# Packed attention with a mixture-of-experts layer: the expert's guess summed on GpSimd, one w2 conversion moved, a branch hint on SyncE, counts read behind the pair turn's copy

## The chip, the cores and the metric

One core of one Trainium2 chip. The metric is the device time in microseconds, the median of several runs; an execution's profile gives its span and what each engine did in it.

## The reference

```python
def sm_attn(qq, kk, vv):                       # per batch (8) and head (8)
    s = scale * qq @ kk.T; s -= s.max(-1)
    a = exp(s); a /= a.sum(-1) + 1e-9
    return a @ vv
packed = sm_attn(p, k, v)                      # 32 packed rows from 576 keys, D = 64
x = sm_attn(q, packed, packed)                 # 576 queries on the 32 packed rows
x = x.transpose(0, 2, 1, 3).reshape(4608, 512)
logits = unit(x) @ unit(expert_emb).T / tau    # 8 experts
e = argmax(logits, axis=1); gate = softmax(logits)[e]
out = gate * (relu(x @ w1[e]) @ w2[e])         # w1: 512 x 1024, w2: 1024 x 512 of expert e
```

All in float32, each token by its own expert.

## The kernel before

The kernel takes the 8 batches (576 tokens each) one after the other and runs two of them interleaved: while TensorE computes the feed-forward products of batch b (`ffn`), steps of the attention of batch b+1 (`att_main`) are put between them. All engines get their instructions in the order in which the Python program emits them (`tc.manual_schedule()`): `ffn` is a generator that yields after each small group of matmuls, and at each yield the main loop runs one step (now and then two) of `att_main(b + 1)` and, from step 21 on, of `gates`. So a step's place in the order of every engine's queue is a matter of how many yields stand ahead of it.

For each batch one expert is guessed: the sum of the packed rows' logits votes, `guess` takes the largest, and its w1 and w2 are loaded for the whole batch. `route` then computes every token's true expert, `counts` how many chose which, and `hits` takes those that chose the guess (`x.sel`) off the batch's 576. At the end all engines load the number of tokens left over (`n_rest`) and branch over a slow second pass (`tc.If(n_rest > 0)`, L1565), which does not run for these inputs. SyncE's branch stands behind its last store.

Weights are used as two parts in a rounded format: `split_w2` makes them by a ScalarE copy (L945) and a GpSimd subtraction (L946), for eight slices of w2 per batch. Four of them are made in the last quarter of the feed-forward product of the batch before (`c == 3`, from `f = 4` on), four in the second half of the hidden layer's steps.

The order of a batch's steps in `ffn` is: hidden layer (L1040, evacuated by ScalarE L1044 and VectorE L1045), the last rows (`h4`, L1075, eight yields, steps 16 to 23), then four groups `c` of 24 matmuls (L1093; group 3 in batch 7 in two halves) with stores. Between them stand, for the next batch: `quarter_scores` (L331), `quarter_values` (L396), the pair turn (L501) and its copy into `x.T` (L570), the row logits (L512, copied by L521), the guess (L631 and the lines behind it, `choose` below), the flips of keys and queries (L291), the query scores (L270), the softmax (`unpack` L677, `biggest` L682, `shift` L688, `total` L697 to L699, `norm` L703, `turn` L706, `low` L717), `route` (L772), and `w1_rows` (L970). `low(0)` runs on GpSimd in batches 2 to 7 ("vvvvpv"). GpSimd's queue also issues the loads of w1 (L927) and w2 (L935) for these batches. `gates` (L889 to L916, with `rsqrt`, L92 to L108) runs on VectorE.

Of the kernel before, what the change touches and what calls it, by code (L numbers as in the profile page):

```python
# [27 lines left out]
def kernel(  # L28
# [54 lines left out]
    ecol = cp.tile([P, E], F32, name="ecol")  # L83
    for e in range(E):
        nc.vector.memset(ecol[:, e : e + 1], float(e))
    rest_f = cp.tile([1, B], F32, name="rest_f")
    rest_i = cp.tile([1, B + 1], I32, name="rest_i")

    def rsqrt(x, y, tag, eng=nc.vector):

        i = sm.tile(list(x.shape), I32, name="rq_i", tag=f"rq_i{tag}", bufs=1)
        nc.vector.tensor_scalar(  # L92
            out=i, in0=x.bitcast(I32), scalar1=-0.5, scalar2=float(0x5F3759DF),
            op0=ALU.mult, op1=ALU.add,
        )
        yield
        hx = sm.tile(list(x.shape), F32, name="rq_h", tag=f"rq_h{tag}", bufs=1)
        eng.tensor_scalar_mul(hx, x, -0.5)
        yield
        t = sm.tile(list(x.shape), F32, name="rq_t", tag=f"rq_t{tag}", bufs=1)  # L100
        cur = i.bitcast(F32)
        for _ in range(3):
            eng.tensor_tensor(out=t, in0=hx, in1=cur, op=ALU.mult)
            yield
            eng.tensor_tensor(out=t, in0=t, in1=cur, op=ALU.mult)
            yield
            if eng is nc.vector:
# [145 lines left out]
    def idle(n):  # L253
        for _ in range(n):
            yield
# [157 lines left out]
    def quarter_sums(x, sums):  # L413
        t = sm.tile([P, NG], F32, name="qr", tag="qr", bufs=1)
        nc.vector.tensor_reduce(t, sums, axis=AX.X, op=ALU.add)
        nc.vector.tensor_scalar(out=t, in0=t, scalar1=1e-9, scalar2=None, op0=ALU.add)
        nc.vector.reciprocal(t, t)
        for g in range(NG):
            x.rinv[g] = t[:, g : g + 1]
# [108 lines left out]
    def att1(x, nat, queries=None, others=()):  # L528

        def pack(queries, others):  # L530
# [23 lines left out]
                counts(other, pt[:1, 256 + n * NC5 * E : 256 + (n + 1) * NC5 * E])  # L554
            next(queries)
            yield
            for other in others:
                counted(other)
                if other is bat[0]:
                    hits(0)  # L560
            quarter_sums(x, sums.rearrange("p (g k) -> p g k", g=NG))
            for g in range(NG):
                pair_rows(x, g, pt[:, g * D : g * D + D])
# [4 lines left out]
            for g in range(NG):  # L568
                pair_turn(x, g, pu)
            nc.vector.tensor_copy(x.T, pu[:, 0 : NG * P])  # L570
            yield from idle(2)
            pt = pc.tile([P, 512], F32, name="pu", tag="pu")
            row_logits(x, pt)
            yield
            logits_out(x, pt)
            next(queries)
            yield

# [39 lines left out]
                drain(asked)  # L618


    def guess(x, late=0, engine=mybir.EngineType.Pool, total=None):
# [12 lines left out]
        yield  # L634
        m8 = sm.tile([1, 8], F32, name="m8", tag="m8", bufs=1)
        idx = sm.tile([1, 8], U32, name="idx", tag="idx", bufs=1)
        nc.vector.max(m8, pt[:1, :E])
        nc.vector.max_index(idx, m8, pt[:1, :E])
# [6 lines left out]
        yield from idle(late)  # L645
        x.e = nc.values_load(
            idx[0:1, 0:1], engines=[engine], min_val=0, max_val=E - 1,
            skip_runtime_bounds_check_because="an index of the largest of E columns",
        )


    def att2(x, after=None, first=False, b1=False, eng1="vvvvvv"):
# [73 lines left out]
        def softmax():  # L726
            order = (
                (unpack, 0), (biggest, 0), (shift, 0), (unpack, 1), (biggest, 1), (total, 0),
                (shift, 1), (norm, 0), (turn, 0), (total, 1), (low, 0), (norm, 1), (turn, 1),
            )  # L730
            if x is bat[1]:
                order = (
# [256 lines left out]
    def ffn(x, store, late=False, after=None, end=False, between=None):  # L989
# [96 lines left out]
        for c in range(4):  # L1086

            w = 256 if end and c == 3 else 512
            for at in range(0, 512, w):
                pf = ps.tile([P, 512], F32, name="pf", tag="pf")  # L1090
                for f in range(NF):
# [8 lines left out]
                    yield  # L1100
                    if f == STF and len(last) > late or f == STF + 3 and late and c == 2:
                        store(*last.pop(0))
                    if c == 3 and f >= 4 and after is not None:
                        split_w2(after)
                    if c == AHEAD and hasattr(after, "lg") and not hasattr(after, "w1g"):
                        after.w1g = w1_rows(after)
# [48 lines left out]
    def att_main(b):  # L1155
        x = bat[b]
        if b:
            if b > 1:
                quarter_banks(x)
            queries = all_queries(x, nat_main(b)) if b > 1 else None  # L1160
            yield from att1(x, nat_main(b), queries, bat[b - 1 if b > 2 else 0 : b] if b > 1 else ())
            sync = b == 1
            queue = nc.sync if sync else nc.gpsimd
            for n, _ in enumerate(guess(
                x, 0 if sync else 2, mybir.EngineType.SP if sync else mybir.EngineType.Pool
            )):
                if n == 1 and queries:
                    next(queries)
                yield
            load_w1(x, x.e, queue=queue)  # L1170
        flips = keys_main(b + 1) if b else None
        second = att2(x, flips, b == 0, b < 1, ENG1 if b == 1 else "vvvvpv")
        if b:
            if b > 1:
                yield
            for _ in range(3 if b == 1 else 2):
                yield next(second)
            load_w2(x, x.e, queue)
        yield from second
        x.soft = True  # L1180
        if b:
            steps = {"r": route(x), "f": flips}
            if b == 1:
                next(flips)
            for turn in TURNS:
                for step in turn:
                    next(steps[step], None)
                yield
        if b == B - 1:
            yield from idle(2)  # L1190
            counts(x)

    def begin():
# [161 lines left out]
        nc.vector.tensor_copy(total, pt[:, :NPR])  # L1355
        both_rows(1)
        queries(0, 0, nc.scalar.copy)
        g_guess = guess(x, 0, mybir.EngineType.SP, total)
        next(g_guess)
        pu = bank()  # L1360
        for g in range(NG):
# [78 lines left out]
    def store_main(b):  # L1440
        x = bat[b]

        def store(c, pf, at, w):
            o = sb.tile([P, DM], F32, name="o", tag="o", bufs=3)
            nc.scalar.activation(o[:, :w], pf[:, :w], AF.Copy, scale=x.gate[:, c : c + 1])  # L1445
            if b == 0:

                for a in range(HB):
# [3 lines left out]
                        rs[:, hf * w + at : hf * w + at + w], o[32 * a : 32 * a + 32, :w]  # L1452
                    )
                return
            rs = out_rows(b, c)
            for a in range(HB):
                n, hf = (a, 0) if c < 4 else (a % 2, a // 2)
# [104 lines left out]
    nc.vector.tensor_reduce(tot, rest_f, axis=AX.X, op=ALU.add)  # L1562
    nc.vector.tensor_copy(rest_i[:, B : B + 1], tot)
    n_rest = nc.values_load(rest_i[0:1, B : B + 1], min_val=0, max_val=B * S)
    with tc.If(n_rest > 0):  # L1565
        with tc.For_i(0, B, 1) as b:
            nb = nc.values_load(rest_i[0:1, ds(b, 1)], min_val=0, max_val=S)
            with tc.If(nb > 0):
# [86 lines left out]
```

## Time and profile before

| | |
|---|---|
| runs | 416.88 us median of 3 (416.35 to 417.67) |
| profiled execution | 416.72 us, span 415.1 us, clock 0.998 |
| busy | PE 403.9 us, PEld 326.1, DVE 307.2, ACT 203.4, POOL 156.7 |
| DMA | 87.93 MB, mean 212 GB/s |

PE is TensorE's matmul side, PEld its weight loads, DVE VectorE, ACT ScalarE, POOL GpSimd, SP SyncE. Times in the views are microseconds from the span's start; "idle before" is the time an engine stood still ahead of a row and what released it. Waits, branches and DMA issues are not counted as busy (a "q" behind the engine's name).

### The profile page before, as it was taken

What the parts mean: (1) busy time and instruction counts of PE and PEld (TensorE: products, weight loads), DVE (VectorE), ACT (ScalarE), POOL (GpSimd) and SP (SyncE); (2) the same over time, 40 slices, a digit from 0 to 9 for tenths busy, and PEclk for the clock granted to TensorE, in tenths of its full rate; (3) what the DMA queues carried; (4) which work ended last, traced back from release to release, by engine and by line L of the source; (5) the groups of instructions that cost most, each with busy time, mean ns of one, the idle gap of its engine ahead of it and who ended that gap; (6) DMA issues with size and microseconds to landing.
All of it is one profiled execution on the core that took longest, in us unless ns stands there. A gap on an engine that the chain in (4) does not pass through costs nothing.

```text
span 415.1 us, 11135 instructions
## 1 busy us (share of the span) xinstructions
PE 403.9 (97%) x4036; PEld 326.1 (79%) x4037; DVE 307.2 (74%) x977; ACT 203.4 (49%) x507; POOL 156.7 (38%) x196
## 2 busy tenths in 40 slices
PE   7999999999999999999999999999999999999993
PEld 3758688797868978698787978689786988779783
DVE  3677889588977889779896889778896798736500
ACT  4677355762357703764147622666038631576110
POOL 2345802437204561056414471046512473142200
PEclk9999999999999999999999999999999999999999
DMA  8999798966989579986999779895899819310021
GB/s 230 334 333 233 205 289 277 238 178 180 309 276 233 144 209 260 308 209 166 247 334 247 183 199 286 302 224 140 236 299 284 199 34 353 119 51 2 20 53 51
DMA packets 42608, 87.93 MB, mean 212 GB/s; under 512 B 11690, under 2 KB 20906, under 8 KB 42546
## 3 DMA queue, kind: packets, MB, share of 16 engines
q1 hardware_dynamic: 35280, 61.44, 53.9%
q0 software_dynamic: 6720, 25.17, 18.9%
q8 instruction: 34, 0.56, 0.6%
q10 hardware_dynamic: 546, 0.54, 0.6%
q14 instruction: 28, 0.23, 0.2%
HBM read 77.68 MB, written 9.44 MB: 210 GB/s over the span
## 4 chain that ended last, share of the span: by engine, by line
PE 92%; DVE 2%; DMA 2%; ACT 1%; POOL 1%; issue 0%; SPq 0%; DVEq 0%; ACTq 0%; POOLq 0%
PE pf L1093 43%; PE pf L1040 23%; PE pf L1075 7%; PE pt L970 3%; PE pt L772 3%; PE pt L270 2%; PE pt L396 2%; PE pt L331 2%; PE pu L772 2%; DMA nat<-in_k 1%; PE pf L1235 1%; PE pt L1267 1%; PE pt L464 1%; DVE hT L1045 0%; PE pf L477 0%
## 5 line engine op out<-in xcount | busy, mean ns | idle before, releaser
L1093 PE MATMUL pf<-w2s,hT 128*128 128x512 f32 (+1 forms) x792 | 181.8, 387 | 0.0
L1093 PEld LDWEIGHTS pf<-w2s,hT 128*128 128x128 f32 x792 | 143.8, 188 | 39.0 <-issue 10.9
L1040 PE MATMUL pf<-AT,G 128*128 128x288 f32 x720 | 102.1, 299 | 0.4 <-DVE hT L1045 0.3
L1040 PEld LDWEIGHTS pf<-AT,G 128*128 128x128 f32 x720 | 97.2, 188 | 4.3 <-issue 1.5
L946 POOL TENSOR_TENSOR w2s<-w2r,w2s 128x512 fp32r<-128x512 f32 x64 | 80.6, 1285 | 50.0 <-ACT w2s L945 50.0
L1045 DVE SCALAR_TENSOR_TENSOR hT<-pf,hT 128x224 fp32r<-128x224 f32 (+1 forms) x128 | 52.3, 414 | 29.9 <-ACT hT L1044 29.6
L1044 ACT ACTIVATE hT<-pf 128x224 fp32r<-128x224 f32 (+1 forms) x128 | 49.2, 385 | 42.8 <-PE pf L1040 40.2
L291 DVE STREAM_TRANSPOSE kt<-nat 128x576 f32<-128x576 f32 x52 | 38.8, 764 | 1.3 <-DMA nat<-in_q 0.6
L1445 ACT ACTIVATE o<-pf,gate 128x512 f32<-128x512 f32 (+1 forms) x41 | 25.9, 633 | 25.7 <-PE pf L1093 14.4
L945 ACT CAST w2s<-w2r 128x512 fp32r<-128x512 f32 x64 | 37.1, 627 | 0.0
L717 POOL TENSOR_TENSOR AT<-at,AT 128x576 fp32r<-128x576 f32 x8 | 11.4, 1421 | 62.2 <-ACT AT L712 62.2
L1075 PE MATMUL pf<-w2r,h 128*64 128x256 f32 x256 | 32.9, 387 | 0.0
L691 ACT ACTIVATE st<-st 128x576 f32<-128x576 f32 (+1 forms) x17 | 11.1, 657 | 37.5 <-DVE st L688 36.4
L983 DVE TENSOR_TENSOR G<-pt,G 128x1024 fp32r<-128x1024 f32 x14 | 16.5, 1220 | 15.7 <-ACT G L982 15.7
L908 ACT ACTIVATE lg<-lg 128x40 f32<-128x40 f32 x8 | 1.9, 236 | 50.7 <-DVE lg L904 50.7
L1075 PEld LDWEIGHTS pf<-w2r,h 128*64 128x64 f32 x256 | 19.5, 137 | 5.1 <-PE pu L501 1.1
L866 POOL MEMSET oh<- 64x8 f32 x8 | 0.8, 98 | 58.5 <-DVE oh L862 58.5
L383 POOL TENSOR_TENSOR qs<-p 128x320 f32<-128x320 f32 x12 | 10.5, 878 | 30.2 <-ACT p L364 30.2
L785 ACT ACTIVATE scr<-pt 128x512 f32<-128x512 f32 (+1 forms) x32 | 15.7, 491 | 12.6 <-DVE part L826 5.8
L712 ACT CAST AT<-at 128x576 fp32r<-128x576 f32 x15 | 10.1, 674 | 23.3 <-DVE at L706 23.2
L364 ACT ACTIVATE p<-pt,qnm 128x160 f32<-128x160 f32 x48 | 17.7, 398 | 0.0
L703 DVE TENSOR_TENSOR st<-st,s 128x576 f32<-128x576 f32 x14 | 16.8, 1202 | 0.3
(229 smaller groups left out, 513.8 us busy)
## 6 DMA issues: line engine op xcount, KB each, us to landing
nat<-in_q SPq DMA_DIRECT2D x112, 140.0 KB, 3.4
nat<-in_k SPq DMA_DIRECT2D x96, 140.0 KB, 4.2
w1t<-in_moe_w POOLq DMA_DIRECT2D x12, 1024.0 KB, 9.7
w2r<-in_moe_w POOLq DMA_DIRECT2D x24, 512.0 KB, 15.8
out<-o SPq DMA_DIRECT2D x124, 64.0 KB, 2.1
w2r<-in_moe_w SPq DMA_DIRECT2D x8, 512.0 KB, 9.7
vn<-in_v SPq DMA_DIRECT2D x24, 160.0 KB, 3.6
vn<-in_v SPq DMA_DIRECT2D x48, 80.0 KB, 3.8
```

Of the source, the lines that this page charges most:

```text
L291: nc.vector.transpose(kt.rearrange("p (c i) -> p c i", i=32), t)
L364: nc.scalar.activation(x.p1[g][:, n * QW : n * QW + QW], area(x, g)[:, n // 2, n % 2], AF.Exp, bias=x.nm[:, at : at + 1],)
L703: eng("N", hf).tensor_tensor(out=t, in0=t, in1=spread(sums[hf], gs), op=ALU.mult)
L772: nc.tensor.matmul(to, x.at[at, g, tokens], x.ppx[at, g], start=True, stop=True, tile_position=(64 * half, column),)
L945: nc.scalar.copy(t[:, 0], raw)
L946: nc.gpsimd.tensor_tensor(out=t[:, 1], in0=raw, in1=t[:, 0].bitcast(F32), op=ALU.subtract)
L1040: nc.tensor.matmul(pf[:, :HS], w, r, start=(n == 0), stop=(n == len(ops) - 1))
L1044: nc.scalar.activation(hT[:, 0, f, cs], pf[:, :n], AF.Relu)
L1045: nc.vector.scalar_tensor_tensor(out=hT[:, 1, f, cs], in0=pf[:, :n], scalar=0.0, in1=hT[:, 0, f, cs].bitcast(F32), op0=ALU.max, op1=ALU.su ...
L1075: nc.tensor.matmul(pf[64 * hf : 64 * hf + 64, :256], h4[:, f], x.w2r[f // 2][:, f % 2, hf * 256 : hf * 256 + 256], start=(f == 0), stop=(f ...
L1093: nc.tensor.matmul(pf[:, :w], hT[:, a, f, c * P : (c + 1) * P], x.w2s[f][:, m, at : at + w], start=(f == 0 and i == 0), stop=(f == NF - 1 ...
L1445: nc.scalar.activation(o[:, :w], pf[:, :w], AF.Copy, scale=x.gate[:, c : c + 1])
```

## The change

- In batches 2 to 7 the row logits of the 128 packed rows are summed by GpSimd (`vote`) instead of by two matmuls; `choose` (largest, its index, `x.sel`) moves from the step behind the guess to the one ahead of the query scores, and the w1 load to the step ahead of the w2 load.
- `counted` and `hits(0)` run behind the copy into `x.T` instead of ahead of the divisors (`quarter_sums`).
- `split_w2(after)` starts at `f = 5`; the slice left over is made behind the last rows, by the loop that was there.
- `low(0)` goes to VectorE and behind `turn(1)`.
- Three `tensor_scalar` of VectorE become `scalar_tensor_tensor` with a second operand in SBUF.
- The branch at the end gets a hint for SyncE, its place being the store of group 2 of the last batch.

```diff
 def rsqrt(x, y, tag, eng=nc.vector):
-        nc.vector.tensor_scalar(
-            out=i, in0=x.bitcast(I32), scalar1=-0.5, scalar2=float(0x5F3759DF),
+        nc.vector.scalar_tensor_tensor(
+            out=i, in0=x.bitcast(I32), scalar=-0.5,
+            in1=magic[: x.shape[0]].broadcast_to(list(x.shape)), op0=ALU.mult, op1=ALU.add,
...
-        eng.tensor_scalar_mul(hx, x, -0.5)
+            eng.scalar_tensor_tensor(out=hx, in0=x, scalar=-0.5, in1=x, op0=ALU.mult, op1=ALU.min)
 def quarter_sums(x, sums):
-        nc.vector.tensor_scalar(out=t, in0=t, scalar1=1e-9, scalar2=None, op0=ALU.add)
+        nc.vector.scalar_tensor_tensor(out=t, in0=t, scalar=1e-9, in1=t, op0=ALU.add, op1=ALU.max)
 def pack(queries, others):
...
             next(queries)
             yield
+            quarter_sums(...); pair_rows(...)
+            yield
+            next(queries)
+            yield
+            pu = ...; pair_turn(x, g, pu); nc.vector.tensor_copy(x.T, pu[:, 0 : NG * P])
+            yield
             for other in others:
                 counted(other)
                 if other is bat[0]:
                     hits(0)
-            (the same lines, and yield from idle(2))
+            yield
             pt = ...; row_logits(x, pt)
             yield
             logits_out(x, pt)
+            if others:
+                vote(x)
             next(queries)
             yield
+    def vote(x):
+        votes = sm.tile([1, NG, E], F32, name="votes", tag="votes", bufs=1)
+        nc.gpsimd.tensor_reduce(votes, x.ppx[:, :, 2 * D :], axis=AX.C, op=ALU.add)
+        x.votes = votes[:, 0]
+        nc.gpsimd.tensor_tensor(out=x.votes, in0=x.votes, in1=votes[:, 1], op=ALU.add)
 def softmax():
-                (shift, 1), (norm, 0), (turn, 0), (total, 1), (low, 0), (norm, 1), (turn, 1),
+                (shift, 1), (norm, 0), (turn, 0), (total, 1), (norm, 1), (turn, 1), (low, 0),
 def ffn(...):
-                    if c == 3 and f >= 4 and after is not None:
+                    if c == 3 and f >= 5 and after is not None:
 def att_main(b):                                    # b > 1
-            (guess: matmuls, yield, choose, next(queries), yield, yield, load_w1)
+                yield
+                next(queries)
+                yield from idle(2)
-        second = att2(x, flips, b == 0, b < 1, ENG1 if b == 1 else "vvvvpv")
+        second = att2(x, flips, b == 0, b < 1, ENG1 if b == 1 else "vvvvvv")
+            yield
+            x.chosen = choose(x, x.votes)
+            yield next(second)                      # the query scores
+            x.e = index_of(x, mybir.EngineType.Pool)
+            load_w1(x, x.e, queue=nc.gpsimd)
+            yield next(second)
+            load_w2(x, x.e, nc.gpsimd)
 def store(c, pf, at, w):
+            if b == B - 1 and c == 2:
+                tc.mark_branch_hint_location("rest", engines=[mybir.EngineType.SP])
-    with tc.If(n_rest > 0):
+    with tc.If(n_rest > 0, label="rest"):
```

## Rows read from the trace of the kernel before

**Rows 1.** Busy time by stretches: stretch, its length, each engine's busy time, PEclk, DMA.
```profile
120.00:170.00 50.00, 50.00 (x505) 40.93 (x504) 41.16 (x126) 25.33 (x65) 19.53 (x24) 1.00 0.83 224
...
400.00:415.00 15.00, 8.65 (x61) 7.96 (x59) 0.00 (x0) 1.63 (x3) 0.00 (x0) 0.96 0.19 48
```
**Rows 2.** Chain of waits, batch 3: start, length, engine, tile, line.
```profile
146.07 0.91 PE pf L1075 x8
...
148.94 1.13 PE pt L270 x32
150.07 15.23 PE pf L1093 x66
```
**Rows 3.** Chain of waits, last rows of batch 7.
```profile
382.73 3.60 PE pf L1075 x32
```
**Rows 4.** Groups of TensorE's instructions by line: busy us, mean ns, idle before.
```profile
L631 PE MATMUL pu<-ppx,equal 128*64 128x8 f32 x28 | 2.5, 196 | 0.0
```
**Rows 5.** Timeline, hand-over to batch 2: start, length, engine, line.
```profile
93.60 0.53 DVE L1437 TENSOR_TENSOR hit<-cnt,sel 1x8 f32<-1x8 f32 x1
...
95.76 0.38 PE L501 MATMUL pu<-ident,ppx 128*128 128x128 f32 x2
...
97.48 0.41 PE L512 MATMUL pu<-enT,T 128*64 128x8 f32 x8 [0.25 <-DVE T L570]
```
**Rows 6.** Timeline of TensorE, hand-over to batch 3.
```profile
144.49 0.38 PE L501 MATMUL pu<-ident,ppx 128*128 128x128 f32 x2
...
145.72 0.35 PE L512 MATMUL pu<-enT,T 128*64 128x8 f32 x8
```
**Rows 7.** Timeline of SyncE from 403 us.
```profile
403.70 6.48 SPq L1459 DMA_DIRECT2D out<-o  x10
```
**Rows 8.** Line 1565: duration ns min/median/max, first and last start us.
```profile
L1565 SPq EVENT_SEMAPHORE  x9: 17/17/17, 412.8 to 413.4; - x9
...
L1565 SPq COMPARE_BRANCH  x1: 50/50/50, 410.2 to 410.2; - x1
```
**Rows 9.** DMA issues from 409 us: KB each, median us to landing.
```profile
out<-o SPq DMA_DIRECT2D x2, 32.0 KB, 1.7
```
**Rows 10.** Timeline of VectorE, batch 3, guess, gates and `unpack`.
```profile
147.20 0.16 DVE L637 MAX8 m<-pu 1x8 f32<-1x8 f32 x1
...
148.72 0.12 DVE L889 TENSOR_TENSOR ss<-sq 128x2 f32<-128x2 f32 x1
...
151.45 0.17 DVE L103 TENSOR_TENSOR rq_t<-rq_h,gy 128x5 f32<-128x5 f32 x1
...
154.36 0.82 DVE L677 STREAM_TRANSPOSE st<-pt 128x288 f32<-128x288 f32 x2
```
**Rows 11.** Timeline of GpSimd, batch 3.
```profile
144.03 3.75 POOL L946 TENSOR_TENSOR w2s<-w2r,w2s 128x512 fp32r<-128x512 f32 x3 [1.17 <-ACT w2s L945]
148.69 1.52 POOL L927 DMA_DIRECT2D w1t<-in_moe_w  x2 [0.92 <-DVE sel L642]
...
162.36 1.42 POOL L717 TENSOR_TENSOR AT<-at,AT 128x576 fp32r<-128x576 f32 x1 [9.34 <-ACT AT L712]
```
**Rows 12.** Part 6 of the page, DMA issues: KB each, median us to landing.
```profile
w1t<-in_moe_w POOLq DMA_DIRECT2D x12, 1024.0 KB, 9.7
```
**Rows 13.** Line 703, VectorE: duration ns min/median/max, first and last start us.
```profile
L703 DVE TENSOR_TENSOR st<-st,s x14: 744/1204/1660, 62.8 to 355.0; 128x576 f32<-128x576 f32 x14
```
**Rows 14.** Timeline ahead of `route`: batches 3 and 5.
```profile
164.44 0.78 DVE L706 STREAM_TRANSPOSE at<-st 128x576 f32<-128x576 f32 x1
...
165.22 1.66 PE L772 MATMUL pt<-ppx,at 64*128 64x136 f32 x24
...
260.28 0.78 DVE L706 STREAM_TRANSPOSE at<-st 128x576 f32<-128x576 f32 x1
...
261.65 0.73 PE L772 MATMUL pt<-ppx,at 64*128 64x136 f32 x8
```
**Rows 15.** Timeline of VectorE, batch 7, gates.
```profile
384.14 0.95 DVE L895 TENSOR_TENSOR ss<-sq 64x1 f32<-64x1 f32 x1
```

More of the change, by code (lines that the diff above doesn't have):

```diff
@@ L85 @@
         nc.vector.memset(ecol[:, e : e + 1], float(e))
+    magic = cp.tile([P, 1], F32, name="magic")
+    nc.vector.memset(magic, float(0x5F3759DF))
     rest_f = cp.tile([1, B], F32, name="rest_f")
@@ L91, in rsqrt @@
         i = sm.tile(list(x.shape), I32, name="rq_i", tag=f"rq_i{tag}", bufs=1)
-        nc.vector.tensor_scalar(
-            out=i, in0=x.bitcast(I32), scalar1=-0.5, scalar2=float(0x5F3759DF),
-            op0=ALU.mult, op1=ALU.add,
+        nc.vector.scalar_tensor_tensor(
+            out=i, in0=x.bitcast(I32), scalar=-0.5,
+            in1=magic[: x.shape[0]].broadcast_to(list(x.shape)), op0=ALU.mult, op1=ALU.add,
         )
@@ L97, in rsqrt @@
         hx = sm.tile(list(x.shape), F32, name="rq_h", tag=f"rq_h{tag}", bufs=1)
-        eng.tensor_scalar_mul(hx, x, -0.5)
+        if eng is nc.vector:
+            eng.scalar_tensor_tensor(
+                out=hx, in0=x, scalar=-0.5, in1=x, op0=ALU.mult, op1=ALU.min
+            )
+        else:
+            eng.tensor_scalar_mul(hx, x, -0.5)
         yield
@@ L415, in quarter_sums @@
         nc.vector.tensor_reduce(t, sums, axis=AX.X, op=ALU.add)
-        nc.vector.tensor_scalar(out=t, in0=t, scalar1=1e-9, scalar2=None, op0=ALU.add)
+        nc.vector.scalar_tensor_tensor(
+            out=t, in0=t, scalar=1e-9, in1=t, op0=ALU.add, op1=ALU.max
+        )
         nc.vector.reciprocal(t, t)
@@ L556, in pack @@
             yield
[L557 to L560, printed above, removed]
             quarter_sums(x, sums.rearrange("p (g k) -> p g k", g=NG))
@@ L570, in pack @@
             nc.vector.tensor_copy(x.T, pu[:, 0 : NG * P])
-            yield from idle(2)
+            yield
+            for other in others:
+                counted(other)
+                if other is bat[0]:
+                    hits(0)
+            yield
             pt = pc.tile([P, 512], F32, name="pu", tag="pu")
@@ L618, in att1, with guess @@
                 drain(asked)
-    def guess(x, late=0, engine=mybir.EngineType.Pool, total=None):
+    def guess(x, total=None):
         pt = pc.tile([P, 512], F32, name="pu", tag="pu")
@@ L634, in guess, with choose @@
         yield
+        x.chosen = choose(x, pt[:1, :E])
+        x.e = index_of(x, mybir.EngineType.SP)
+    def choose(x, votes):
         m8 = sm.tile([1, 8], F32, name="m8", tag="m8", bufs=1)
         idx = sm.tile([1, 8], U32, name="idx", tag="idx", bufs=1)
-        nc.vector.max(m8, pt[:1, :E])
-        nc.vector.max_index(idx, m8, pt[:1, :E])
+        nc.vector.max(m8, votes)
+        nc.vector.max_index(idx, m8, votes)
         gi = sm.tile([1, 1], F32, name="gi", tag="gi", bufs=1)
@@ L644, in guess, with index_of @@
         )
-        yield from idle(late)
-        x.e = nc.values_load(
-            idx[0:1, 0:1], engines=[engine], min_val=0, max_val=E - 1,
+        return idx
+    def index_of(x, engine):
+        return nc.values_load(
+            x.chosen[0:1, 0:1], engines=[engine], min_val=0, max_val=E - 1,
             skip_runtime_bounds_check_because="an index of the largest of E columns",
         )
+    def vote(x):
[3 more added lines that the diff above has]
+        nc.gpsimd.tensor_tensor(out=x.votes, in0=x.votes, in1=votes[:, 1], op=ALU.add)
     def att2(x, after=None, first=False, b1=False, eng1="vvvvvv"):
@@ L1161, in att_main @@
             yield from att1(x, nat_main(b), queries, bat[b - 1 if b > 2 else 0 : b] if b > 1 else ())
[L1162 to L1168, printed above, removed]
+            if b == 1:
+                for _ in guess(x):
+                    yield
+                load_w1(x, x.e)
+            else:
                 yield
-            load_w1(x, x.e, queue=queue)
+                next(queries)
+                yield from idle(2)
         flips = keys_main(b + 1) if b else None
-        second = att2(x, flips, b == 0, b < 1, ENG1 if b == 1 else "vvvvpv")
[L1173 to L1176, printed above, removed]
-                yield next(second)
-            load_w2(x, x.e, queue)
+        second = att2(x, flips, b == 0, b < 1, ENG1 if b == 1 else "vvvvvv")
+        if b == 1:
+            for _ in range(3):
+                yield next(second)
+            load_w2(x, x.e)
+        elif b:
+            yield
[5 more added lines that the diff above has]
+            load_w2(x, x.e, nc.gpsimd)
         yield from second
@@ L1357, in begin @@
         queries(0, 0, nc.scalar.copy)
-        g_guess = guess(x, 0, mybir.EngineType.SP, total)
+        g_guess = guess(x, total)
         next(g_guess)
```

## The prediction

> **What bounds the kernel now.** I read the table by stretches first. TensorE is busy 50.00 of 50 us in each of the five stretches from 120 to 370 us, at the full granted clock, 1.00 of 2.4 GHz [rows 1]. So between the start and the last matmul only two things count: instructions that TensorE no longer has to run, and the few places where it is late. VectorE and GpSimd matter only where a matmul waits for them. Then the end: in the stretch from 400 to 415 us TensorE works 8.65 us [rows 1]; the other 6.35 us are the tail behind the last matmul. The diff touches four places: the guess of the expert in batches 2 to 7 (six times), the hand-over from batch 1 to batch 2, VectorE's softmax chain ahead of `route`, and the branch behind the last store. For the first I read the chain of waits, for the others the timeline of the engines.
>
> **1. The guess leaves TensorE (gain 1.0 us).** Per batch, the two products of L631 run as four matmuls. In the chain, the stretch from the end of the row logits to the first query score holds 24 matmuls of L1075 and these four: 146.07 to 148.94, 2.87 us [rows 2]. Batch 7's own rows have no L631 among them and take 3.60 us for 32, or 0.1125 us each [rows 3]; 24 of them are 2.70 us. The four cost 0.17 us, six times 1.0 us. From below: the eight L1075 at 146.07 go at 0.114 us each [rows 2], which makes 24 of them 2.73 and leaves 0.14 us, 0.8 in all. From above: all L631 matmuls are busy 2.5 us for 28 [rows 4], 2.1 us for 24. I take 1.0, because it compares whole stretches. Nothing of TensorE's waits for the vote: the query scores need the turned queries, whose last flip comes earlier, as `choose` no longer sits ahead of it.
>
> **2. Counts behind the copy (gain 0.5 us, once).** In batch 2 two counts are read and `hits(0)` runs ahead of the divisors on VectorE; one of its instructions alone, L1437, takes 0.53 us [rows 5]. The copy into `x.T` is late by that, and TensorE idles 0.25 us ahead of L512 for it [rows 5]. From the pair turn (L501) to the row logits (L512) it takes 97.48 - 95.76 = 1.72 us in batch 2 [rows 5], and 145.72 - 144.49 = 1.23 us in batch 3, where TensorE shows no idle [rows 6]. The difference, 0.49 us, goes, since these instructions now run behind the copy. What is late next is L512's own place behind eight L1075 matmuls. Batches 3 to 7 read one count each, and L512 does not hold TensorE there: nothing. Bounds: 0.25 (the idle alone) to 0.6.
>
> **3. The branch at the end (gain 1.9 us).** SyncE issues its last store until 410.18 (403.70 + 6.48) [rows 7]. It branches at 410.2 for 0.05 us and runs nothing until 412.8, over 2.5 us; then come nine semaphore waits, 412.8 to 413.4, some 0.07 us each [rows 8]. The ten issues in 6.48 us put the last one at about 409.7, and SyncE's last stores land 1.7 us after their issue [rows 9]: about 411.5 us. So the stall outlasts the landing. If the hint brings the target in during the 6.5 us of stores behind the mark, the nine waits (0.6 us) run beside the landing and the last one passes at 411.5 instead of 413.4: 1.9 us. The rest of the tail moves with it. Bounds: nothing, if the hint does not reach this branch, to 2.0 us. I take the upper part, because the fetch has over twice its time.
>
> **4. The vote on GpSimd (no price, if it fits).** GpSimd is in the last of three w2 subtractions when the row logits are ready; they end at 147.78 (144.03 + 3.75) [rows 11], so the reduction starts at about 147.8. VectorE, without `choose` (from 147.20 to the flip and the gates' start at 148.72, less that flip of 0.7: 0.8 us [rows 10]), begins the gates at about 147.9. By the order of the steps, two steps of gates stand ahead of `choose` in its new place: 13 instructions, 148.72 to 151.62 now [rows 10], 2.9 us with a stall of some 0.5 beside the w1 load's issue, which no longer falls there: 2.4. So `choose` comes up at about 150.3, and a vote of up to 2.5 us is hidden. No row shows a reduction across partitions. Bounds from the nearest rows of GpSimd: below, nothing; above, the elementwise 128x576 of 1.42 us [rows 11]. I take 1.4, the longest row that reads all partitions, and nothing for the path. Behind `choose` wait the rest of the gates and `unpack` on VectorE, and in GpSimd's own queue the w1 and w2 loads: they slip by some 3 us (148.69 [rows 11] to about 151.7). w1 lands 9.7 us after its issue [rows 12], at 161.4, and is used behind 72 matmuls of L1093, which go at 0.231 us each (15.23 for 66 from 150.07 [rows 2]): not before 166.7. So the slip is covered.
>
> The Trainium skill ("GPSIMD Engine Reference", section 3.2) measures 247,699 ns for a reduction along partitions of [128, 2048], 121 ns a column. An estimate from it for these 16 columns is 1.9 us, also under 2.5, so this item would stay at nothing by it.
>
> **5. The w2 conversion behind the last rows (no price).** One subtraction of 1.25 us (3.75 for three) follows the vote on GpSimd, to about 150.6. Its product is used in the last eighth of the first group of L1093, 21 matmuls behind 150.07: 154.9 us [rows 2, 11]. Cover: over 4 us.
>
> **6. `low(0)` on VectorE, behind `turn(1)` (slack, no time by itself).** `norm` takes between 0.74 and 1.66 us [rows 13]; the long one is the second, ahead of the last L706, exactly while GpSimd's `low(0)` runs (162.36, 1.42 us [rows 11]). With that gone, the last transpose ends 0.9 us earlier. It now ends at 165.22 in batch 3, where `route`'s matmuls start at 165.22, and at 261.06 in batch 5, where they start at 261.65 [rows 14]. So the margin is 0 to 0.6 us and becomes 0.9 to 1.5. `low(0)`, at most the 0.9 us won, falls behind that point.
>
> **7. `scalar_tensor_tensor` for `tensor_scalar`.** Each is one instruction for one, inside VectorE's slack: nothing; if a stall goes, that adds to the margin of item 6.
>
> **Sum.** 1.0 + 0.5 + 1.9 = 3.4 us. The profiled execution took 416.72 us for its span of 415.1, and 1.6 us lie around the span; it is 0.16 us under the median of 416.88. I predict 416.88 - 3.4 = 413.5 us.
>
> **Rivals.**
> *A. The hint does nothing* (the target is fetched only at the branch, as now). Then 1.5 us remain: 415.4 us. For it: the only fetch in the rows is the stall itself. Against: 6.5 us of stores lie between mark and branch.
>
> *B. The vote and the conversion behind it hold VectorE, and TensorE becomes late at `route`: slower.* While GpSimd runs an elementwise instruction, VectorE's small ones with operands in SBUF stand still: beside w2 subtractions L1437 takes 0.53 us [rows 5] and batch 7's L895 0.95 us [rows 15], where their like take 0.12 to 0.17 [rows 10]. Place: the gates' first 13 instructions, which now fall into the vote. If they are held through vote and conversion, they start at 147.8 + 1.4 + 1.25 = 150.5 and end at 152.9; `choose` (0.8) ends at 153.7, the rest of the gates (151.62 to 154.36 [rows 10], 2.7 us) at 156.4. `unpack` starts then instead of at 154.36, 2.1 us late; 0.9 comes back through item 6. The margin of 0 to 0.6 us is overdrawn by 0.6 to 1.2 us a batch, 4.5 us over six at a middle value: 418.0 us. It decides from a vote of about 0.5 us; each further microsecond costs six. Against it: VectorE can get in between two GpSimd instructions, as L895's wait is shorter than one subtraction, and the STT forms leave fewer stalls.
>
> The Trainium skill's rule speaks for B ("SBUF — State Buffer", section "Who interferes with whom"): a VectorE instruction with two SBUF inputs contends with a GpSimd one that reads SBUF, and the second to issue is blocked for all of the first. The rows of L895 and `norm` agree; whether a reduction holds the port throughout, no row here shows. With the skill's 1.9 us as the vote, B would come to about 421 us.
>
> *C. The order of flips, counts, gates and loads costs elsewhere*: a flip that its transfer does not reach in time, or w2 late for the next batch's first conversion. At 0.2 to 0.5 us a batch it gives back 1 to 3 us: 415 to 416.5. Against: the margins of items 4 and 5 are several microseconds.
>
> **How the numbers follow.** A measurement of this kernel tells about 0.3% from no change, here 1.25 us: faster is under 415.6, slower over 418.1. The forecast has 0.60 (all faster; its own range 411.9 to 414.6). A has 0.15, at the border, 0.09 faster and 0.06 same. B has 0.18, spread from 416 to 424: 0.12 slower, 0.06 same. C has 0.07: 0.03 faster, 0.04 same. So faster 0.72, same 0.16, slower 0.12. The low end, 411.9, is 2.0 us for the tail, 0.6 for batch 2 and the 2.1 of the guess, with 0.3 for a stall gone. The high end, 417.5, holds A, C and a third of B; some 0.13 of B lies above it and 0.05 of the forecast below the low end.
>
> **What would show it.** Item 1: no L631 outside batch 1, and the end of L512 to L270 shorter by 0.1 to 0.3 us a batch. Item 2: L501 to L512 in batch 2 at 1.23 us. Item 3: SyncE's nine waits starting within 0.5 us of its branch, the last one at the landing. Items 4 and 6: the reduction's time on GpSimd, the second `norm` near 0.75 us, and the last L706 ending before `route`'s matmuls are up. Wrong would be: TensorE idle ahead of `route` in batches 2 to 7, or a fetch stall still there behind SyncE's branch.

## The result, and the profile after

The changed kernel takes 413.0 us (median of 6 runs, 412.49 to 413.71) against 417.04 us of the kernel before (median of 6, the three of the first table among them): a ratio of 0.9898, 95% interval 0.9881 to 0.9914. 413.5 had been predicted. The profiled execution took 413.71 us for its span of 412.0; before, 416.72 for 415.1. The two spans differ by 3.1 us, and that difference is accounted for here. The profiled execution of the changed kernel happened to have a start 0.8 us longer than that of the kernel before; without it the spans differ by 3.9, near the 4.0 between the medians.

The stretches of the changed kernel that answer to [rows 1]:
```profile
120.00:170.00 50.00, 50.00 (x502) 40.50 (x501) 42.24 (x132) 25.93 (x67) 20.35 (x25) 1.00 0.83 243
...
400.00:412.00 12.00, 7.54 (x56) 7.02 (x55) 0.00 (x0) 1.63 (x3) 0.00 (x0) 1.00 0.19 49
```
TensorE is still busy throughout at the full granted clock; what changed lies in what it has to run and in the tail, the time from the end of the last matmul to the end of the span.

TensorE ahead of batch 3's query scores, timeline before and after; the ends overlap, so I compare starts:
```profile
145.72 0.35 PE L512 MATMUL pu<-enT,T 128*64 128x8 f32 x8
145.92 1.06 PE L1075 MATMUL pf<-w2r,h 128*64 128x256 f32 x8
146.81 0.29 PE L631 MATMUL pu<-ppx,equal 128*64 128x8 f32 x3
...
147.01 1.92 PE L1075 MATMUL pf<-w2r,h 128*64 128x256 f32 x15
148.87 1.20 PE L270 MATMUL pt<-kt,T 64*32 64x288 f32 x32
```
```profile
145.71 0.35 PE L521 MATMUL pu<-enT,T 128*64 128x8 f32 x8
145.91 2.79 PE L1100 MATMUL pf<-w2r,h 128*64 128x256 f32 x24
148.63 1.20 PE L277 MATMUL pt<-kt,T 64*32 64x288 f32 x32
```
From the row logits to the query scores it took 148.87 - 145.72 = 3.15 us and now takes 148.63 - 145.71 = 2.92: 0.23 us a batch, not 0.17. The chain shows the 24 matmuls between them as one row:
```profile
146.07 2.64 PE pf L1100 x24
...
149.84 15.18 PE pf L1118 x66
```

The hand-over to batch 2, to [rows 5]:
```profile
96.52 0.38 PE L510 MATMUL pu<-ident,ppx 128*128 128x128 f32 x2
...
97.74 0.35 PE L521 MATMUL pu<-enT,T 128*64 128x8 f32 x8
...
98.13 0.48 DVE L1467 TENSOR_TENSOR hit<-cnt,sel 1x8 f32<-1x8 f32 x1
```
The turn to the logits takes 1.22 us (1.72 before), without idle; `hits(0)` runs behind them.

SyncE's branch and its nine waits, to [rows 8] (duration ns; first and last start):
```profile
L1597 SPq EVENT_SEMAPHORE  x9: 17/17/17, 409.5 to 410.3; - x9
L1597 SPq COMPARE_BRANCH  x1: 70/70/70, 409.0 to 409.0; - x1
```
From the branch to the first wait: 0.5 us instead of 2.6. The last wait passes at 410.3. ScalarE issues its last store at 408.54 us, and it lands 1.7 us later; the eighth of SyncE's waits passes at 410.25, right behind that landing, and the rest of the tail is the same closing sequence as before, 1.7 us. So the landing of the last store is now what the end waits for. It does so by little: the other waits follow each other by 0.1 us, and without the landing the last one would pass some 0.2 us earlier.

GpSimd and VectorE in batch 3, to [rows 10] and [rows 11]:
```profile
147.74 2.02 POOL L672 CROSS_LANE_REDUCE votes<-ppx 128x16 f32<-128x16 f32 x1
149.84 0.22 POOL L674 TENSOR_TENSOR votes<-votes 1x8 f32<-1x8 f32 x1
153.00 1.28 POOL L971 TENSOR_TENSOR w2s<-w2r,w2s 128x512 fp32r<-128x512 f32 x1 [2.93 <-ACT w2s L970]
154.22 1.52 POOL L952 DMA_DIRECT2D w1t<-in_moe_w  x2
```
```profile
148.36 0.17 DVE L94 SCALAR_TENSOR_TENSOR rq_i<-ss,magic 128x5 int32<-128x5 int32 x1
148.63 0.17 DVE L110 TENSOR_TENSOR rq_t<-rq_h,rq_i 128x5 f32<-128x5 f32 x1
150.10 0.16 DVE L653 MAX8 m<-votes 1x8 f32<-1x8 f32 x1
153.28 1.01 DVE L1467 TENSOR_TENSOR hit<-cnt,sel 1x8 f32<-1x8 f32 x1
154.41 0.82 DVE L702 STREAM_TRANSPOSE st<-pt 128x288 f32<-128x288 f32 x2
```
The reduction takes 2.02 us, the votes are ready at 150.06, and `choose` starts at 150.10. While the reduction runs, the gates' small instructions take 0.17 us each. `unpack` starts at 154.41, as before (154.36). But the left-over w2 conversion stands still for 2.93 us and runs at 153.00.

Where the 3.1 us between the spans went, stretch by stretch (a batch's start is its first `route` matmul):

| stretch | before | after | difference |
|---|---|---|---|
| start to batch 1 | 68.24 | 69.01 | +0.77 |
| batch 1 to batch 2 | 48.77 | 47.99 | -0.78 |
| batch 2 to batch 7 | 240.95 | 239.75 | -1.20 |
| batch 7 to the last matmul's end | 50.69 | 50.79 | +0.10 |
| tail behind it | 6.46 | 4.47 | -1.99 |

The first row is not the work of the change: this stretch varied from 67.7 to 69.9 us in the other profiles, two of which (68.1 and 69.9) had the kernel before's own start.

### The profile page after: what moved, and what is told of

Its sections match the earlier page's. It is cut to its first block, busy times and chain, and to the rows that moved or that the text cites. A ratio compares the mean times of both kernels' runs of the same rounds, so it can differ in the third digit from the quotient of the medians.

```text
span 412.0 us, 11101 instructions
## 1 busy us (share of the span) xinstructions
PE 403.6 (98%) x4012; PEld 322.5 (78%) x4013; DVE 310.5 (75%) x984; ACT 203.6 (49%) x507; POOL 161.7 (39%) x202
## 4 chain that ended last, share of the span: by engine, by line
PE 89%; DMA 7%; SPq 1%; issue 0%; DVE 0%; ACT 0%; DVEq 0%; ACTq 0%
PE pf L1118 43%; PE pf L1065 22%; PE pf L1100 6%; PE pt L995 3%; PE pt L797 3%; DMA w2r<-in_moe_w 2%; DMA vn<-in_v 2%; PE pt L403 2%; DMA nat<-in_q 2%; PE pt L277 2%; PE pt L338 2%; PE pu L797 2%; PE pf L1253 1%; PE pf L1265 1%; SPq L952 0%
## 5 line engine op out<-in xcount | busy, mean ns | idle before, releaser
L1100 PE MATMUL pf<-w2r,h 128*64 128x256 f32 x256 | 31.5, 385 | 0.0
L1100 PEld LDWEIGHTS pf<-w2r,h 128*64 128x64 f32 x256 | 16.9, 137 | 8.5 <-PE pu L510 1.0
L960 POOL DMA_DIRECT2D w2r<-in_moe_w x24 | 17.0, 721 | 0.0
L702 DVE STREAM_TRANSPOSE st<-pt 128x288 f32<-128x288 f32 x32 | 13.3, 451 | 0.9 <-PE pt L1297 0.9
```

The lines of the kernel that those rows point to most:

```text
L960: queue.dma_start(t, w2e[:, 2 * i : 2 * i + 2, :])
L1100: nc.tensor.matmul(pf[64 * hf : 64 * hf + 64, :256], h4[:, f], x.w2r[f // 2][:, f % 2, hf * 256 : hf * 256 + 256], start=(f == 0), stop=(f ...
```

## The experiments

In each the "batch time" is the time from one batch's first `route` matmul to the next one's: 48.15 to 48.23 us before and 47.93 to 47.97 after, except 48.77 and 47.99 for the step to batch 2. The kernels of this section ran in three later groups of runs, each beside the kernel before (416.69, 416.96 and 416.94 us), which its ratio is against; so a difference of some tenths between the medians of two changed kernels can come from the group.

### The hint alone, and all but the hint

```diff
 # kernel before
+            if b == B - 1 and c == 2:
+                tc.mark_branch_hint_location("rest", engines=[mybir.EngineType.SP])
-    with tc.If(n_rest > 0):
+    with tc.If(n_rest > 0, label="rest"):
```


> The kernel before with the branch hint alone. Theory (a fetch stall behind SyncE's branch, hidden by the hint): the time falls by 2.0 us, to a ratio of 0.995; SyncE's nine waits start about 0.5 us behind its branch instead of 2.6, and from the last matmul's end to the span's end it is 4.5 us instead of 6.4. Rival (the tail is set by the landing of the last stores and by the other engines): the waits start earlier but end where they did, and the ratio is 1.000.

414.58 us, ratio 0.995 (0.9937 to 0.9964); tail 4.47 us. The second kernel is the changed one without these lines:

> The changed kernel without the branch hint. Theory: 2.0 us slower than the changed kernel, 415.0 us, 0.995 of the time before; the tail behind the last matmul is 6.4 us again. Rival (the shorter tail came with other code ahead of the branch, which shifted its place among the fetched blocks): the tail stays at 4.5 us and the ratio at 0.990.

415.17 us, ratio 0.9964 (0.9947 to 0.998); tail 6.27 us. Its branch and waits:
```profile
L1595 SPq EVENT_SEMAPHORE  x9: 17/17/17, 410.2 to 410.8; - x9
L1595 SPq COMPARE_BRANCH  x1: 50/50/50, 407.7 to 407.7; - x1
```
2.5 us between them again. The hint takes 2.1 us off the kernel before and is worth 2.2 in the changed one (415.17 - 413.0); by the tails alone it is 2.0 and 1.8. So it is worth about 2 us with or without the other changes. The hint works on this branch, by taking the stall from behind it. What SyncE does during the stall no row shows: that it fetches the target's instructions is the prediction's reading, and these runs do not test it.

### Counts alone, and all but the counts

```diff
 # kernel before, pack(); the second kernel is the changed one with this undone
-            for other in others:
-                counted(other)
-                if other is bat[0]:
-                    hits(0)
             quarter_sums(...)
...
             nc.vector.tensor_copy(x.T, pu[:, 0 : NG * P])
-            yield from idle(2)
+            yield
+            (the loop over others, as above)
+            yield
```


> The kernel before with the counts read behind the copy, nothing else. Theory: in batch 2 the pair turn to the row logits takes 1.23 us instead of 1.72, TensorE shows no idle there, and 0.5 us is gained once, a ratio of 0.999, too little for the time itself to show. Rival (GpSimd's subtraction that runs beside it holds the divisors as long): 1.72 us stays, since the copy waits for the same point.

416.18 us, ratio 0.9983 (0.9967 to 1.0). The turn to the logits fell to 1.22 us, but the next stretch, to the query scores, grew from 3.20 to 3.39, as the guess on TensorE now waited for the logits' copy, which stands behind the counts:
```profile
99.99 0.25 PEld L632 LDWEIGHTS pu<-ppx,equal 128*64 128x64 f32 x3 [0.47 <-DVE ppx L521]
```
The step to batch 2 took 48.53 us, a net 0.24.

> The changed kernel with the counts read ahead of the divisors again. Theory (item 2): in batch 2 the pair turn to the row logits takes 1.72 us instead of 1.22 and the cadence from batch 1's route to batch 2's is 48.45 instead of 47.97; 0.5 us slower, 413.5 us, ratio 0.991. Rival (the copy waits for GpSimd's subtraction in either order): 1.22 us stays.

413.86 us, ratio 0.9933 (0.9914 to 0.9952): the step to batch 2 took 48.52 us against 47.99, and the idle is back:
```profile
95.99 0.38 PE L510 MATMUL pu<-ident,ppx 128*128 128x128 f32 x2
...
97.71 0.41 PE L521 MATMUL pu<-enT,T 128*64 128x8 f32 x8 [0.25 <-DVE T L579]
```
So the move is worth 0.5 us with the guess off TensorE, and half of it with the guess still there.

### The guess back on TensorE

```diff
 # changed kernel, pack()
-            if others:
-                vote(x)
# and att_main(b > 1)
+                pt = pc.tile([P, 512], F32, name="pu", tag="pu")
+                for g in range(NG):
+                    nc.tensor.matmul(pt[:64, :E], equal, x.ppx[:, g, 2 * D :], ...)
+                x.votes = pt[:1, :E]
                 yield
```


> The changed kernel with the guess summed by TensorE again, all else left (choice ahead of the query scores, hint, counts, one conversion behind the last rows). Theory (the four matmuls a batch cost TensorE 0.25 us, by the cadence of the batches, 48.21 before and 47.95 after): 1.5 us slower than the changed kernel, 414.5 us, ratio 0.9935. By the prediction's own size, 0.17 us each, it is 1.0 us: 414.0. Rival (the shorter cadence comes from VectorE's or GpSimd's part, not from TensorE's matmuls): the cadence stays at 47.95 us and the ratio at 0.990.

415.12 us, ratio 0.9971 (0.9954 to 0.9987). Logits to query scores take 3.15 us again (3.39 in batch 2), and from batch 1 to batch 7 it is 289.53 us against 287.73: 1.8 us for the guess, of which 6 x 0.23 = 1.4 are the four small matmuls and 0.24 the wait in batch 2 that the counts' new place makes. The last 0.16 fell into one batch step (48.34 us); its cause was not looked for.

### The vote twice as long, with and without the conversion behind it

```diff
 # changed kernel, vote(); for the second kernel also the other line
         nc.gpsimd.tensor_reduce(votes, x.ppx[:, :, 2 * D :], axis=AX.C, op=ALU.add)
+        nc.gpsimd.tensor_reduce(votes, x.ppx[:, :, 2 * D :], axis=AX.C, op=ALU.add)
-                    if c == 3 and f >= 5 and after is not None:
+                    if c == 3 and f >= 4 and after is not None:
```


> The changed kernel with the reduction across partitions run twice, 4.0 us instead of 2.0. Theory: the vote fitted with almost no room; now the choice comes 2.0 us later, the gates' exponential on ScalarE with it, behind that the last w2 conversion, and its product is ready at about 156.3 in batch 3's clock where TensorE wants it at 154.7. TensorE idles about 1.6 us in the first group of L1118 in each of six batches: 9.6 us slower than the changed kernel, 422.6 us, ratio 1.013. By item 4 of the prediction with item 5's cover of over 4 us, only VectorE's chain is late, and TensorE idles ahead of route: 2.0 less the margin of 0.6, six times, 8.4 us. Rival (the whole hand-over has slack of several microseconds): no change, 413.0.

422.52 us, ratio 1.0146 (1.0112 to 1.018); the batch times rose to 49.49 to 49.58 us, 1.6 a batch for 2.0 more of vote. TensorE stands still inside the first group of the last feed-forward product:
```profile
154.53 0.24 ACT L934 ACTIVATE lg<-lg 128x40 f32<-128x40 f32 x1 [8.66 <-DVE lg L930]
154.67 0.60 ACT L971 CAST w2s<-w2r 128x512 fp32r<-128x512 f32 x1
...
155.35 1.27 POOL L972 TENSOR_TENSOR w2s<-w2r,w2s 128x512 fp32r<-128x512 f32 x1 [2.93 <-ACT w2s L971]
...
156.68 10.27 PE L1119 MATMUL pf<-w2s,hT 128*128 128x512 f32 x44 [0.85 <-POOL w2s L972]
```
GpSimd's subtraction waits for ScalarE's cast, the cast stands behind the gates' exponential (L934) in ScalarE's queue, the exponential waits for the gates on VectorE (L930), which stand behind `choose`, and `choose` waits for the vote.

> Both: the reduction twice, and no conversion left behind the last rows. Theory (the conversion is what makes a long vote dear): TensorE idles only ahead of route, 2.0 us less a margin of 0.6 and less the 0.9 that VectorE no longer waits, about 0.5 us in six batches: 3 us slower than the changed kernel, 416 us. If VectorE's chain alone decides in both, it is 8 us with the conversion and 3 without, and the idle time stands ahead of route in both.

417.06 us, ratio 1.0 (0.998 to 1.0021), batch times 48.53 to 49.04. Without the conversion behind it, the longer vote costs nothing in the step to batch 2 (47.99 us) and 0.6 to 1.1 us in each of the other five, at another place:
```profile
165.07 1.67 PE L798 MATMUL pt<-ppx,at 64*128 64x136 f32 x24
165.17 0.78 DVE L732 STREAM_TRANSPOSE at<-st 128x576 f32<-128x576 f32 x1
168.99 0.25 DVE L817 TENSOR_REDUCE lg<-pt 128x8 f32<-128x32 f32 x2
171.90 0.18 PEld L996 LDWEIGHTS pt<-w1t,T 64*32 64x32 f32 x16 [1.04 <-ACT scr L811]
```
`route`'s matmuls start ahead of the last transpose's end without a wait (their first ones do not need it). It is `w1_rows` that idles, for the squares that ScalarE makes when VectorE has evacuated `route`; that began at 168.99 us. In the changed kernel it begins at 167.40:
```profile
164.95 1.31 PE L797 MATMUL pt<-ppx,at 64*128 64x136 f32 x18
167.40 0.25 DVE L816 TENSOR_REDUCE lg<-pt 128x8 f32<-128x32 f32 x2
170.36 0.18 PEld L995 LDWEIGHTS pt<-w1t,T 64*32 64x32 f32 x16 [0.35 <-ACT scr L810]
```
The 0.35 us of idle here are weight loads, whose matmuls were not late. Counted from `route`'s start the evacuation comes at 3.92 us with the vote doubled and at 2.45 in the changed kernel. Of the loss, 0.3 to 0.65 us fall at `w1_rows`; the rest, about 0.5 in batch 3, falls behind it, at the quarter scores, the hidden layer and the quarter values.

### The conversion in its old place

The changed kernel with `f >= 4` alone:

> The changed kernel with the w2 conversions from f = 4 on again, so that none is left behind the last rows. Theory: GpSimd's subtraction at 153 us goes, VectorE's L1467 loses its wait (1.01 us to 0.15), unpack starts 0.9 us earlier, and TensorE, which waited for neither, gains nothing: 413.0 us, ratio 0.990. Rival (the conversion was moved because w2 lands too late for it at f = 4): TensorE or ScalarE waits there, 0.5 us or more a batch, 416 us.

412.97 us, ratio 0.9918 (0.9888 to 0.9948): the changed kernel's time. Counted from the batch's start, `unpack` comes 0.6 us earlier in batch 3, and `hits` takes 0.15 us instead of 1.01, but TensorE's batch time is 47.95 either way. So the move of the conversion bought no time that these runs show. It has a small price: from batch 7 to the last matmul's end it takes 50.69 us in all six profiles with `f >= 4`, the kernel before's among them, and 50.79 in all eight with `f >= 5`.

### Shorter vote

```diff
 # changed kernel, vote()
+        nc.gpsimd.tensor_tensor(out=both, in0=x.ppx[:, 0, 2 * D :], in1=x.ppx[:, 1, 2 * D :], op=ALU.add)
-        nc.gpsimd.tensor_reduce(votes, x.ppx[:, :, 2 * D :], axis=AX.C, op=ALU.add)
+        nc.gpsimd.tensor_reduce(votes, both, axis=AX.C, op=ALU.add)
-        nc.gpsimd.tensor_tensor(out=x.votes, in0=x.votes, in1=votes[:, 1], op=ALU.add)
```


> The changed kernel with the two halves of the row logits added first (128 x 8), then reduced over 8 columns instead of 16. Theory (the reduction's time goes by its columns): 1.0 us instead of 2.0, with about 0.2 us for the sum. The votes are ready at 149.1 instead of 150.06; the choice still comes up at 150.1 behind the gates, so the time stays: 413.0 us, ratio 0.990. Rival (a fixed price of the instruction): 2.0 us again, the votes 0.1 us later, and no change in the time either; the row of the reduction tells them apart.

413.43 us, ratio 0.9918 (0.9898 to 0.9937): no gain, although the reduction is shorter by 0.9 us. `choose` starts at 149.89 us in batch 3 (150.10 in the changed kernel; this kernel's batch 3 runs 0.04 us earlier). So in the changed kernel it waited for the votes, by 0.17 us, and not only for the gates ahead of it, as had been expected; TensorE did not wait for those 0.17. The groups by line (busy us, mean ns, idle), of the changed kernel and of this one:
```profile
L672 POOL CROSS_LANE_REDUCE votes<-ppx 128x16 f32<-128x16 f32 x6 | 12.1, 2010 | 0.0
```
```profile
L676 POOL CROSS_LANE_REDUCE votes<-both 128x8 f32<-128x8 f32 x6 | 6.8, 1125 | 0.5
```

### `low(0)` back on GpSimd

```diff
 # changed kernel
-                (shift, 1), (norm, 0), (turn, 0), (total, 1), (norm, 1), (turn, 1), (low, 0),
+                (shift, 1), (norm, 0), (turn, 0), (total, 1), (low, 0), (norm, 1), (turn, 1),
-ENG1 if b == 1 else "vvvvvv")
+ENG1 if b == 1 else "vvvvpv")
```


> The changed kernel with low(0) on GpSimd again, between total(1) and norm(1). Theory (item 6: it holds the second norm): norm takes 1.66 us instead of 0.76, the last transpose ends 0.9 us later, 0.3 us past the point at which route's matmuls now start, and TensorE idles there: 0.3 us in six batches, 2 us slower than the changed kernel, 415 us, ratio 0.995. Rival (as before, the margin can be nothing without TensorE waiting): no change, 413.0, ratio 0.990.

413.29 us, ratio 0.9923 (0.9892 to 0.9953). `norm` is long again and the last transpose ends behind `route`'s start. In batch 3 it does so by 0.3 us, and TensorE is not late:
```profile
163.85 1.65 DVE L728 TENSOR_TENSOR st<-st,s 128x576 f32<-128x576 f32 x1
165.54 0.78 DVE L731 STREAM_TRANSPOSE at<-st 128x576 f32<-128x576 f32 x1
166.02 1.66 PE L797 MATMUL pt<-ppx,at 64*128 64x136 f32 x24
```
The same holds for batches 4 to 7 (0.27 to 0.45 us behind; batch times 47.93 to 47.95). In batch 2, where `route` starts at 117.71, the transpose ends 0.63 us behind it:
```profile
117.56 0.78 DVE L731 STREAM_TRANSPOSE at<-st 128x576 f32<-128x576 f32 x1
...
121.10 0.25 DVE L816 TENSOR_REDUCE lg<-pt 128x8 f32<-128x32 f32 x2
...
124.30 0.18 PEld L995 LDWEIGHTS pt<-w1t,T 64*32 64x32 f32 x16 [1.00 <-ACT scr L810]
```
VectorE begins to evacuate `route` 3.39 us behind its start (3.03 to 3.22 in batches 3 to 6, 1.71 in batch 7), and half of `w1_rows` comes 0.3 us late: the step from batch 2 to batch 3 took 48.31 us. So the theory, a loss in each of six batches ahead of `route`, fell. The slack is needed once, in batch 2, at `w1_rows`, for about 0.3 us, which the medians are too coarse to show.

### `tensor_scalar` again

```diff
 # changed kernel, rsqrt(); the same for hx and in quarter_sums()
-        nc.vector.scalar_tensor_tensor(out=i, in0=x.bitcast(I32), scalar=-0.5, in1=magic..., ...)
+        nc.vector.tensor_scalar(out=i, in0=x.bitcast(I32), scalar1=-0.5, scalar2=float(0x5F3759DF), ...)
```


> The changed kernel with the tensor_scalar forms back in rsqrt and quarter_sums. Theory (item 7 of the prediction, one instruction for one): the gates' two stand beside the reduction across partitions, which did not hold the scalar_tensor_tensor forms nor any two-input instruction (0.16 us each), so they take 0.17 us there too: 413.0 us, ratio 0.990. Rival (the reduction holds VectorE's tensor_scalar, as the w1 load's issue did before): the first of them ends with the reduction, 1.3 us late, the choice and the last w2 conversion slip by as much, and TensorE idles 0.9 us ahead of the 22nd matmul of L1118 in six batches: 418.4 us, ratio 1.003.

416.53 us, ratio 0.9998 (0.9982 to 1.0014): 3.5 us over the changed kernel; against the kernel before, nothing measurable is left of the gain. VectorE and GpSimd in batch 3:
```profile
148.04 2.01 POOL L665 CROSS_LANE_REDUCE votes<-ppx 128x16 f32<-128x16 f32 x1
148.65 1.43 DVE L94 TENSOR_SCALAR rq_i<-ss 128x5 int32<-128x5 int32 x1
148.73 1.36 DVE L100 TENSOR_SCALAR rq_h<-ss 128x5 f32<-128x5 f32 x1
154.30 1.29 POOL L964 TENSOR_TENSOR w2s<-w2r,w2s 128x512 fp32r<-128x512 f32 x1 [3.94 <-ACT w2s L963]
```
The two `tensor_scalar` end with the reduction, at 150.08 and 150.09 us (it ends at 150.05); the whole chain from the gates to the conversion slips. The conversion starts at 154.30 us instead of 153.00; 0.3 of these 1.3 us is this execution's longer start, so the slip is 1.0 us. TensorE waits for the conversion six times (batch times 48.53 to 48.59).

### Two stores in place of four at the end

```diff
 # changed kernel with f >= 4, store(), last piece of batch 7
+            if at:
+                for a, queue in ((0, nc.sync), (2, nc.scalar)):
+                    queue.dma_start(
+                        rs[:, a : a + 2, at : at + w].rearrange("i n m -> n i m"),
+                        o[32 * a : 32 * a + 64, :w])
+                return
```


> The changed kernel with the conversions from f = 4 on and the very last piece stored by two transfers of 64 partitions, one from SyncE and one from ScalarE, instead of two each. Theory (with the branch hidden, the span ends by the landing of the last stores, which are issued 0.36 to 0.43 us behind the first ones): the last landing and the nine waits end 0.4 us earlier, the tail behind the last matmul is 4.1 us instead of 4.5, 412.6 us, ratio 0.989. Rival (a transfer of 64 partitions takes as much longer to issue and to land): the tail stays at 4.5 us.

416.87 us, ratio 1.0007 (0.9993 to 1.0022): both theory and rival missed, since the tail grew to 8.02 us. The issues take 0.69 and 0.63 us, and the last wait passes at 412.8, over 5 us behind the issue:
```profile
L1604 SPq EVENT_SEMAPHORE  x9: 17/17/17, 408.4 to 412.8; - x9
```
The stretches of its transfers, and one of the changed kernel with its four stores (last three columns: granted clock, DMA share of 16 engines, GB/s):
```profile
408.00:410.00 2.00, 0.00 (x0) 0.00 (x0) 0.00 (x0) 0.00 (x0) 0.00 (x0) 1.00 0.15 36
410.00:412.00 2.00, 0.00 (x0) 0.00 (x0) 0.00 (x0) 0.00 (x0) 0.00 (x0) 0.55 0.13 39
```
```profile
408.00:410.00 2.00, 0.00 (x0) 0.00 (x0) 0.00 (x0) 0.10 (x1) 0.00 (x0) 1.00 0.25 67
```
A share of 0.13 to 0.15 of 16 engines is about two engines' worth. The Trainium skill ("DMA: Bandwidth & Descriptors", section "Rules for kernel authors") has it that an outermost dimension of fewer than 16 confines a transfer to at most that many engines; here, in the output's access pattern, it is 2. The share agrees with that, but no run changed the outermost dimension alone, so the cause is not shown.

## Why the prediction was right, and where its steps were off

The sum was 1.0 + 0.5 + 1.9 = 3.4 us; the terms measured 1.4 + 0.5 + 2.0 = 3.9, with 0.1 lost in the last stretch. Three gains were named and three were found, each where it had been placed; what was off lies in one size and in what was to cost nothing.

- **Item 1 was mis-sized**: 0.23 us a batch, not 0.17. I had priced the 24 matmuls between logits and query scores at batch 7's 0.1125 us; alone they take 2.64 us, 0.110 each. A rate borrowed from another batch made an error of a third in a difference this small, inside the bounds of 0.8 to 2.1. The experiment with the guess put back shows the same 0.23 a batch, 3.15 us against 2.92, and adds the 0.24 in batch 2.
- **Item 2 was right** (0.49 predicted; 0.50 in the trace, 0.53 in the batch time), but only together with item 1, which I had not seen: alone it gets half (48.53 us against 48.77).
- **Item 3 was right**: the stall outlasted the landing, and without it the landing decides, by some 0.2 us. Rival A is refuted by both experiments on the hint. The fetch that the item speaks of stays an assumption.
- **Item 4 was right, but by luck of size**: the vote took 2.02 us plus 0.22 where I took 1.4, and VectorE would have come to `choose` at about 149.9 us, earlier than the 150.3 that I had worked out. So the vote did not fit: `choose` waited 0.17 us for it, as the shorter vote shows, and started at 150.10. The wait cost nothing, thanks to the cover of item 5. An estimate from the Trainium skill ("GPSIMD Engine Reference", section 3.2) was 1.9 us and was nearer than the row that I took. The room is used up: 2 us more cost 1.6 a batch. The w1 load slipped to 154.22 instead of 151.7, and nothing waited for it.
- **Item 5 named the wrong wait.** I let the conversion follow the vote, to 150.6 us, with over 4 us of cover. It needs ScalarE's cast too, which stands behind the gates' exponential and so behind `choose`; it ended at 154.28. The 22nd matmul of the group uses the cast's product and the 23rd the subtraction's: that one starts at 154.88, and with the vote doubled it is the one that waits for GpSimd (156.68). The cover is 0.6 us. It was enough, so the term stayed zero; with the vote doubled, or with `tensor_scalar`, it was not.
- **Item 6 located the margin wrongly, and its size too.** I measured it from the last transpose to `route`'s start and expected 0.9 to 1.5 us; in the changed kernel it is 0.26 us in batch 2 and 0.6 in batches 3 to 7, since `hits`, held to 1.01 us beside the conversion that item 5 had moved, puts `unpack` off (with the conversion in its old place the margin is 1.0 to 1.5). What decides is when VectorE evacuates `route`, since the squares and `w1_rows` hang on it: with `low(0)` on GpSimd again an evacuation up to 3.22 us behind `route`'s start cost nothing, and one at 3.39 cost 0.3 us, once, in batch 2. So the slack bought that 0.3, not a term in every batch.
- **Item 7 was wrong**: "nothing" is right for one instruction against one, but with the vote beside them the old forms cost 3.5 us. The swap is what makes the vote free. Of the three swapped instructions the two of the gates are seen to be held; the third was not put back by itself.
- **Rival B** went the other way round. The instructions with two operands in SBUF, which I had feared for, ran at 0.17 us beside the reduction; the `tensor_scalar` of one operand were held to its end. The Trainium skill ("SBUF — State Buffer", section "Who interferes with whom") names instructions with two SBUF operands as contending with a GpSimd one that reads SBUF, and counts `tensor_scalar` among those that can, in some modes. The experiment agrees for `tensor_scalar`; for two operands the trace disagrees beside this reduction and agrees beside the w2 subtraction (`hits`, 1.01 us), and the measurement decides. The kernel with `tensor_scalar` back came near to B's 418 us (416.5), by conversion and cast and not at `route`, B's place. (B's price holds a slip of its own: the middle of 0.6 to 1.2 us is 0.9, six times that is 5.4, so 418.9 and not 418.0.)
- **Rival C** was not seen: the batch times of 47.93 to 47.97 leave no room for it.

## What to carry over

When work is moved to an idle engine, follow each thing that it makes late through the queues of the other engines to the next instruction that the bound engine needs: here the vote's deadline lay at the end of vote, `choose`, gates, a ScalarE cast and a GpSimd subtraction, 0.6 us away, not in the 4 us seen on GpSimd alone. Which instructions of a neighbour can run beside the moved work is a matter of their form, and swapping the form first can decide the sign. A branch at the end of a kernel deserves a look at what its engine does between the branch and its next instruction.

## What the runs showed of the hardware

- GpSimd's reduction over 128 partitions takes 2.01 us for 16 columns and 1.125 for 8; if its time is linear in the columns, that is 0.11 us a column and about 0.24 besides.
- Beside it VectorE's `tensor_scalar` of 128x5 in SBUF took 1.36 and 1.43 us in batch 3, each ending with the reduction, its `scalar_tensor_tensor` 0.17.
- SyncE's branch without a hint was followed by 2.5 us of nothing, with it by 0.5.
- The start up to batch 1 took between 67.7 and 69.9 us in the profiles of this case, though the kernels' starts are the same or nearly so; what makes it vary was not tried.
